# Where and when the second layer's inputs are loaded and split in a two-layer fp32 MLP behind a retention block

## Chip, cores and metric

One core of a Trainium2 chip. The metric is the device time of one execution in microseconds (us), the median of several runs; lower is better.

## What is computed

Attention without a softmax (a decay matrix `Dmat` takes its place), then two feed-forward layers, all in float32. Cut from the reference, with the shapes put in:

```python
q, k, v: [4, 8, 576, 64]
scores = (1 / sqrt(64)) * q @ k.T
ret = scores * Dmat                       # Dmat[h, i, j] = gamma[h] ** (i - j) for i >= j, else 0
x = (ret @ v) -> [2304, 512]
h = x @ w_in                              # first layer, w_in [512, 2048]
x = (h * sigmoid(h)) @ w_out              # w_out [2048, 512]
h = x @ w_in2                             # second layer, the same shapes
out = (max(h, 0) ** 2) @ w_out2           # [2304, 512]
```

## The kernel before

**Tiling.** The 2304 tokens are cut into five blocks (`BLOCKS`: 512, 384, 384, 512, 512). The main loop runs over `(layer, j, f)`: layer 0 with its five blocks `j`, then layer 1 with its five; in each block sixteen steps `f`, one for each group of 128 hidden units. In a step, `gemm1` multiplies the block's input by 128 columns of the first weight into a PSUM tile `ph`; `gate` applies the nonlinearity; `gemm2`, two steps later (`LAG`), adds that group's part into the accumulators `acc`. Every float32 factor is held as a rounded part and a rest (`xh` and `xl`, `gh` and `gl`, `wh` and `wl`), and three products are summed (line 74). A step of a 512-token block is thus 12 matmuls of `gemm1` and 12 of `gemm2`.

**The work beside the matmuls.** For each step ScalarE applies the sigmoid or relu (L380, L383) and casts `gh` (L388); VectorE multiplies (L381, L384) and subtracts `gl` (L389). The weights come as packed 64-bit words `wr`, through three buffers, and are converted by both engines: ScalarE L101, L102 and the cast L121; VectorE L107, L108, L109 and the subtraction L125. `conv_to` works a unit of half a step's weights at a time and mixes three units: while unit i has its L101 and L102, unit i-1 has its L107 to L109, and unit i-2 its L121 and L125. SyncE's queue issues a weight load (L92) as soon as the L109 that frees its buffer is done. The second layer's weights are converted over layer 0's last block and layer 1's first, about nine units in eight steps.

**Order.** Each engine takes its instructions in the order in which the program emits them; it is written out by hand. A function put into `later` is emitted at the next `flush()`, of which there are two in a step, each after a call of `conv_to`. So the gate of a step follows the first of them, the cast of `gh` the second, and the subtraction of `gl` the first of the step after.

**Between the layers.** Each block's output of layer 0 is copied to `y` and written to the DRAM tile `x2[j]` from ScalarE's queue (L433). `load_x2(j)` (lines 435 to 444) reads it back into the tile `xr` from SyncE's queue (L438), and directly behind it emits four ScalarE casts to `xh` (L442) and four VectorE subtractions to `xl` (L443). It is called at step 8 of layer 0's last block for block 0, and at step 4 of each block of layer 1 for the block after it: five calls. `xr` and the output tile `y` share two buffers and take turns in them.

Of the kernel before, what the change touches and what calls it, by code (L numbers as in the profile page):

```python
# [7 lines left out]
F32 = mybir.dt.float32  # L8
F32R = mybir.dt.float32r
# [15 lines left out]
KD, KF = DM // 128, DFF // 128  # L25
BLOCKS = [512, 384, 384, 512, 512]
NBMAX = max(BLOCKS)
LAG = 2
W1_FIRST, W1_AHEAD = 6, 5
ST_W = (0, 1, 1, 2)  # L30
ST_C = (0, 0, 1, 2, 2, 3, 3, 4, 4)
W2_LAG, W2_NUM, W2_DEN = 0, 9, 8
HALF = (slice(0, 64), slice(64, 128))
RAW = 3
# [4 lines left out]
def kernel(  # L39
# [16 lines left out]
    nc = tc.nc  # L56
# [4 lines left out]
    xp = ctx.enter_context(tc.tile_pool(name="xp", bufs=2))  # L61
# [67 lines left out]
    later = []  # L129

    def flush():
        now = later[:]
        later.clear()
        for emit in now:
            emit()
# [5 lines left out]
    def load_next():  # L141
        if n_loaded[0] < load_end[0]:
            load_w(n_loaded[0])
            n_loaded[0] += 1

    def conv_to(layer, n):

        for i in range(conv_n[layer], min(n, 2 * KF + 2)):
            conv_n[layer] += 1
            for lag, stage in ((2, conv_c), (0, conv_a), (1, conv_b), (2, conv_d)):  # L150
                if 0 <= i - lag < 2 * KF:
                    stage(layer * 2 * KF + i - lag)
                    if stage is conv_b and n_loaded[0] < i - lag + layer * 2 * KF + RAW + 1:
                        load_next()
# [200 lines left out]
    x2 = [dp.tile([128, KD, n], F32, name=f"x2_{j}") for j, n in enumerate(BLOCKS)]  # L355
    tok0 = [sum(BLOCKS[:j]) for j in range(len(BLOCKS))]
    late = {}

    def gemm1(layer, j, f):
        n = BLOCKS[j]  # L360
        ph = ps_g.tile([128, 512], F32, tag="g", name="ph")[:, 0:n]
        wh, wl = wt[layer, f]
        xh, xl = x_t[j] if layer == 0 else late["x", j]
        for k in range(KD):
            w0 = slice(k * 128, k * 128 + 128)
            mm3(
                ph,
                [(wh[:, w0], xh[:, k, 0:n]), (wh[:, w0], xl[:, k, 0:n]), (wl[:, w0], xh[:, k, 0:n])],
                first=k == 0,
                last=k == KD - 1,  # L370
            )
        later.append(lambda: gate(layer, j, f, ph))
# [60 lines left out]
                    q.dma_start(out=to, in_=y[:, 0:w])  # L433

    def load_x2(j):
        n = BLOCKS[j]
        r = late["pool"].tile([128, KD, n], F32, tag="xr", name="xr")
        nc.sync.dma_start(out=r, in_=x2[j])  # L438
        xh = xp.tile([128, KD, NBMAX], F32R, tag="xh", name="xh")[:, :, 0:n]
        xl = xp.tile([128, KD, NBMAX], F32R, tag="xl", name="xl")[:, :, 0:n]  # L440
        for k in range(KD):
            nc.scalar.copy(xh[:, k], r[:, k])  # L442
            nc.vector.tensor_sub(xl[:, k], r[:, k], xh[:, k])  # L443
        late["x", j] = (xh, xl)


    nb = len(BLOCKS)
# [34 lines left out]
    def run_att(upto, su=False):  # L482
        while pos[0] < min(upto, len(steps)):
            steps[pos[0]][1](su)
            pos[0] += 1

    def att_end(j):
        last = u_end[j] - 1
        return max(i for i, s in enumerate(steps) if s[0] <= last) + 1

    e0 = att_end(0)
    for i in range(1, e0 + 1):
        run_att(i, True)
        conv_to(0, ST_C[i])
        flush()
# [8 lines left out]
    for i in range(len(seq) + LAG):  # L504
        if i < len(seq):
            layer, j, f = seq[i]
            gemm1(layer, j, f)
        for half in range(2):
            if layer == 0 and j == 0:
                conv_to(0, 2 * f + half + 1 + W1_AHEAD)  # L510
            elif i > w2_base + W2_LAG:
                conv_to(1, (2 * (i - w2_base - W2_LAG) + half - 1) * W2_NUM // (2 * W2_DEN))
            flush()
            if half and i >= LAG:
                gemm2(*seq[i - LAG])
            if i < len(seq) and layer == 0 and j + 1 < nb:
                a0, a1 = att_end(j), att_end(j + 1)
                run_att(a0 + (a1 - a0) * (2 * f + half + 1) // (2 * KF - 3))
        if i < len(seq):
            if layer == 0 and j == nb - 1 and f == 0:  # L520
                ap_ctx.close()
                load_end[0] = 4 * KF
                for _ in range(RAW):
                    load_next()
                late["pool"] = ctx.enter_context(tc.tile_pool(name="lp", bufs=2))
            if layer == 0 and j == nb - 1 and f == KF - 8:
                load_x2(0)
            if layer == 1 and f == 4 and j + 1 < nb:
                load_x2(j + 1)


# [54 lines left out]
```

## Time and profile before

| what | value |
|---|---|
| median of 3 runs | 898.37 us (897.97 to 899.33) |
| the profiled execution's own time | 897.14 us |
| span of its trace | 895.4 us |
| TensorE matmul (PE) busy | 862.8 us, 96% of the span |
| VectorE (DVE) busy | 427.6 us, 48% |
| ScalarE (ACT) busy | 327.1 us, 37% |
| mean granted TensorE clock | 0.982 |

The trace is of one execution, 1.2 us shorter than the median of the runs. Its times count from the start of the span, which leaves 1.7 us of that execution's time outside. PE is TensorE's matmuls, SP is SyncE, which only issues transfers here; SPq and ACTq mark the DMA issues of the two queues. The end of a matmul is modelled in the trace, and neighbours overlap in it; the starts are the better measure.

### The profile page before, as it was taken

How to read it: one execution, taken by the hardware profiler on the slowest of the kernel's cores; microseconds unless marked ns; L12 is line 12 of the kernel's file. 1: busy time of each engine (PE TensorE's matmuls, PEld its weight loads, DVE VectorE, ACT ScalarE, POOL GpSimd, SP SyncE). 2: the span in 40 equal slices, each digit the busy share in tenths (PEclk: the TensorE clock that was granted, in tenths of full speed). 3: DMA queues.
4: the chain of work that ended last, by engine and by line, in shares of the span. 5: the costliest groups of instructions: out<-in, count | busy, mean ns of one | idle time of the engine just before them, and what ended most of it. 6: DMA issues, size and time to landing. Idle time of an engine off the chain costs nothing.

```text
span 895.4 us, 14028 instructions
## 1 busy us (share of the span) xinstructions
PE 862.8 (96%) x5930; PEld 739.8 (83%) x5930; DVE 427.6 (48%) x722; ACT 327.1 (37%) x594; POOL 72.8 (8%) x105
## 2 busy tenths in 40 slices
PE   6698979999999999999999989999999999999998
PEld 5576758999999888888878878889999888888886
DVE  3899995333443333335767776632242233223222
ACT  3576663222222322225556555432232223222221
POOL 5210111111122021100000000000000000000000
PEclk8699999999999999999999999999999999999999
DMA  9445532111211213002343433020020020001001
GB/s 355 175 140 191 181 127 95 48 48 48 84 49 48 84 48 118 1 1 95 120 139 118 142 131 115 2 83 1 1 83 1 0 83 1 1 0 48 1 1 47
DMA packets 21662, 68.27 MB, mean 76 GB/s; under 512 B 2400, under 2 KB 4192, under 8 KB 21216
## 3 DMA queue, kind: packets, MB, share of 16 engines
q1 hardware_dynamic: 17280, 59.91, 19.5%
q10 hardware_dynamic: 4320, 7.47, 2.3%
q8 instruction: 46, 0.75, 0.3%
q14 instruction: 16, 0.13, 0.0%
HBM read 57.93 MB, written 9.44 MB: 75 GB/s over the span
## 4 chain that ended last, share of the span: by engine, by line
PE 82%; DVE 2%; DMA 1%; issue 0%; ACT 0%; SPq 0%; ACTq 0%
PE acc L74 40%; PE ph L74 39%; PE Q L301 2%; DMA xr<-x 1%; PE P L250 1%; PE P L255 1%; DVE xl L443 0%; DVE t L108 0%; DVE gl L389 0%; DVE t L109 0%; DVE t L107 0%; DVE wl L125 0%; PE Q L317 0%; ACT xh L442 0%; SPq L92 0%
## 5 line engine op out<-in xcount | busy, mean ns | idle before, releaser
L74 PE MATMUL ph<-xh,wh 128*128 128x512 f32 (+1 forms) x640 | 238.1, 372 | 5.6 <-ACT xh L335 5.6
L74 PE MATMUL ph<-xl,wh 128*128 128x512 f32 (+1 forms) x640 | 236.4, 369 | 0.0
L74 PE MATMUL ph<-xh,wl 128*128 128x512 f32 (+1 forms) x640 | 236.3, 369 | 0.0
L384 DVE SCALAR_TENSOR_TENSOR sg<-ph,sg 128x512 f32<-128x512 f32 (+1 forms) x80 | 51.0, 638 | 195.3 <-ACT sg L383 195.3
L74 PEld LDWEIGHTS ph<-xh,wh 128*128 128x128 f32 x640 | 120.8, 189 | 24.0 <-ACT xh L335 5.8
L74 PEld LDWEIGHTS ph<-xl,wh 128*128 128x128 f32 x640 | 120.7, 189 | 16.8 <-DVE xl L336 0.4
L74 PEld LDWEIGHTS ph<-xh,wl 128*128 128x128 f32 x640 | 120.7, 189 | 15.2
L74 PE MATMUL acc<-gl,wh 128*128 128x512 f32 (+1 forms) x320 | 120.2, 376 | 9.6 <-DVE gl L389 9.4
L389 DVE TENSOR_TENSOR gl<-sg,gh 128x512 fp32r<-128x512 f32 (+1 forms) x160 | 103.5, 647 | 52.9 <-ACT gh L388 52.6
L388 ACT CAST gh<-sg 128x512 fp32r<-128x512 f32 (+1 forms) x160 | 92.3, 577 | 91.2 <-DVE sg L384 51.5
L381 DVE TENSOR_TENSOR sg<-ph,sg 128x512 f32<-128x512 f32 (+1 forms) x80 | 50.9, 636 | 148.7 <-ACT sg L380 148.7
L74 PE MATMUL acc<-gh,wh 128*128 128x512 f32 (+1 forms) x320 | 120.5, 377 | 0.0
L383 ACT ACTIVATE sg<-ph 128x512 f32<-128x512 f32 (+1 forms) x80 | 44.5, 556 | 207.9 <-PE ph L74 207.5
L74 PE MATMUL acc<-gh,wl 128*128 128x512 f32 (+1 forms) x320 | 119.0, 372 | 0.0
L74 PE MATMUL acc<-wh,gl 128*128 128x512 f32 x288 | 112.8, 392 | 2.8 <-DVE gl L389 2.8
L74 PE MATMUL acc<-wl,gh 128*128 128x512 f32 x288 | 112.6, 391 | 0.0
L74 PE MATMUL acc<-wh,gh 128*128 128x512 f32 x288 | 112.0, 389 | 0.0
L380 ACT ACTIVATE sg<-ph 128x512 f32<-128x512 f32 (+1 forms) x80 | 44.3, 554 | 159.0 <-PE ph L74 159.0
L74 PEld LDWEIGHTS acc<-gl,wh 128*128 128x128 f32 x320 | 60.8, 190 | 21.3 <-DVE gl L389 13.9
L74 PEld LDWEIGHTS acc<-gh,wh 128*128 128x128 f32 x320 | 60.6, 189 | 8.7
L74 PEld LDWEIGHTS acc<-gh,wl 128*128 128x128 f32 x320 | 60.9, 190 | 7.4
L74 PEld LDWEIGHTS acc<-wh,gl 128*128 128x128 f32 x288 | 54.1, 188 | 14.6 <-DVE gl L389 3.2
(50 smaller groups left out, 738.0 us busy)
## 6 DMA issues: line engine op xcount, KB each, us to landing
wr<-w SPq DMA_DIRECT2D x64, 512.0 KB, 3.5
raw<-att SPq DMA_DIRECT2D x34, 512.0 KB, 5.3
x<-y ACTq DMA_DIRECT2D x12, 256.0 KB, 2.5
xr<-x SPq DMA_DIRECT2D x3, 1024.0 KB, 5.5
out<-y SPq DMA_DIRECT2D x10, 256.0 KB, 2.1
out<-y ACTq DMA_DIRECT2D x7, 256.0 KB, 2.3
x<-y ACTq DMA_DIRECT2D x8, 192.0 KB, 1.9
xr<-x SPq DMA_DIRECT2D x2, 768.0 KB, 5.3
```

The lines of the kernel that those rows point to most:

```text
L74: mm(o, a, b, start=first and i == 0, stop=last and i == n - 1)
L250: mm(o, dims(u, a, e, b, 768), dims(u, a, e, b, 0), start=True, stop=True)
L255: mm(o, toks(u, a, e, b, 256), toks(u, a, e, b, 512), start=True, stop=True)
L301: mm(w, a, b, start=e not in started, stop=last)
L380: nc.scalar.activation(s, ph, ACTF.Sigmoid)
L381: nc.vector.tensor_mul(s, ph, s)
L383: nc.scalar.activation(s, ph, ACTF.Relu)
L384: nc.vector.scalar_tensor_tensor(s, ph, 0.0, s, op0=ALU.max, op1=ALU.mult)
L388: nc.scalar.copy(gh, s)
L389: later.append(lambda: nc.vector.tensor_sub(gl, s, gh))
```

## The change

The load is issued from ScalarE's queue in place of SyncE's, at step 4 of the block before (`X2_LOAD`), for block 0 too, where it was step 8. The casts and subtractions are taken out of `load_x2` into `split_x2`, which is called at the end of steps 10 to 13 (`X2_SPLIT`), one cast each; the subtraction goes into `later`, so it is emitted at the first flush of the next step, behind that step's subtraction of `gl`.

```diff
+X2_LOAD, X2_SPLIT = 4, 10
...
     def load_x2(j):
-        n = BLOCKS[j]
-        r = late["pool"].tile([128, KD, n], F32, tag="xr", name="xr")
-        nc.sync.dma_start(out=r, in_=x2[j])
-        xh = xp.tile([128, KD, NBMAX], F32R, tag="xh", name="xh")[:, :, 0:n]
-        xl = xp.tile([128, KD, NBMAX], F32R, tag="xl", name="xl")[:, :, 0:n]
-        for k in range(KD):
-            nc.scalar.copy(xh[:, k], r[:, k])
-            nc.vector.tensor_sub(xl[:, k], r[:, k], xh[:, k])
-        late["x", j] = (xh, xl)
+        r = late["pool"].tile([128, KD, BLOCKS[j]], F32, tag="xr", name="xr")
+        nc.scalar.dma_start(out=r, in_=x2[j])
+        late["r", j] = r
+
+    def split_x2(j, k):
+        n, r = BLOCKS[j], late["r", j]
+        if k == 0:
+            late["x", j] = tuple(
+                xp.tile([128, KD, NBMAX], F32R, tag=nm, name=nm)[:, :, 0:n] for nm in ("xh", "xl")
+            )
+        xh, xl = late["x", j]
+        nc.scalar.copy(xh[:, k], r[:, k])
+        later.append(lambda: nc.vector.tensor_sub(xl[:, k], r[:, k], xh[:, k]))
...
-            if layer == 0 and j == nb - 1 and f == KF - 8:
-                load_x2(0)
-            if layer == 1 and f == 4 and j + 1 < nb:
-                load_x2(j + 1)
+            nxt = j + 1 if layer else 0
+            if (layer == 1 or j == nb - 1) and nxt < nb:
+                if f == X2_LOAD:
+                    load_x2(nxt)
+                if X2_SPLIT <= f < X2_SPLIT + KD:
+                    split_x2(nxt, f - X2_SPLIT)
```

## Rows read from the trace of the kernel before

**Rows 1.** The profile's page: busy time of each engine (share of the span), instructions.

```profile
PE 862.8 (96%) x5930; PEld 739.8 (83%) x5930; DVE 427.6 (48%) x722; ACT 327.1 (37%) x594; POOL 72.8 (8%) x105
```

**Rows 2.** Waits, 440 to 530 us: total us, times, longest us.

```profile
ACT xh L442 <- DMA xr<-x: 12.1, 2, 6.4
DVE xl L443 <- ACT xh L442: 11.4, 2, 6.1
...
PE acc L74 <- DVE gl L389: 4.7, 2, 2.8
```

**Rows 3.** Busy time by stretch, layer 1's second block: us, engines, PEclk, DMA share, GB/s.

```profile
578.00:650.00 72.00, 72.00 (x363) 65.17 (x362) 21.58 (x40) 19.63 (x40) 0.00 (x0) 1.00 0.08 26
```

**Rows 4.** Timeline of PE, first stall: start, us, instruction, idle before and releaser.

```profile
453.99 0.39 PE L74 MATMUL acc<-gh,wh 128*128 128x512 f32 x1
456.24 0.50 PE L74 MATMUL acc<-gl,wh 128*128 128x512 f32 x1 [1.87 <-DVE gl L389]
...
460.46 0.39 PE L74 MATMUL ph<-xh,wh 128*128 128x512 f32 x1
```

**Rows 5.** Timeline of PE, second stall.

```profile
523.04 0.39 PE L74 MATMUL acc<-wh,gh 128*128 128x512 f32 x1
...
526.48 0.50 PE L74 MATMUL acc<-wh,gl 128*128 128x512 f32 x1 [2.83 <-DVE gl L389]
...
528.89 0.39 PE L74 MATMUL ph<-xh,wh 128*128 128x512 f32 x1
```

**Rows 6.** The chain that ended last: an undisturbed group of twelve matmuls.

```profile
463.37 2.72 PE acc L74 x12
```

**Rows 7.** Busy time by stretch, the matmuls right after the first stall.

```profile
458.00:460.46 2.46, 2.46 (x8) 1.89 (x7) 2.46 (x5) 1.85 (x4) 0.00 (x0) 0.56 0.29 40
```

**Rows 8.** Timeline of ACT, at the first stall and at the second.

```profile
452.44 2.18 ACT L442 CAST xh<-xr 128x512 fp32r<-128x512 f32 x4 [6.38 <-DMA xr<-x]
454.53 0.59 ACT L380 ACTIVATE sg<-ph 128x512 f32<-128x512 f32 x1
...
520.92 1.75 ACT L442 CAST xh<-xr 128x384 fp32r<-128x384 f32 x4 [5.75 <-DMA xr<-x]
522.58 0.62 ACT L121 CAST wh<-t 128x512 fp32r<-128x512 f32 x1
```

**Rows 9.** Tile xr: ns min/median/max, first and last start; landing us min/median/max.

```profile
L442 ACT CAST xh<-xr x20: 507/614/620, 452.4 to 740.0; 128x512 fp32r<-128x512 f32 x12, 128x384 fp32r<-128x384 f32 x8
L443 DVE TENSOR_TENSOR xl<-xr,xh x20: 550/684/693, 453.1 to 740.9; 128x512 fp32r<-128x512 f32 x12, 128x384 fp32r<-128x384 f32 x8
L438 SPq DMA_DIRECT2D xr<-x x5: 377/405/469, 446.9 to 724.0; - x5
...
DMA to landing us min/median/max: 4.9/5.5/5.7
```

**Rows 10.** The layer-0 output writes that ScalarE's queue issues: ns min/median/max.

```profile
L433 ACTq DMA_DIRECT2D x<-y x20: 326/327/1324, 152.5 to 503.0; - x20
```

**Rows 11.** Timeline of DVE around step 4 of layer 0's last block.

```profile
424.03 0.69 DVE L109 SCALAR_TENSOR_TENSOR t<-wr,t 128x512 int32<-128x512 int32 x1
...
427.72 0.68 DVE L389 TENSOR_TENSOR gl<-sg,gh 128x512 fp32r<-128x512 f32 x1
...
438.50 0.69 DVE L381 TENSOR_TENSOR sg<-ph,sg 128x512 f32<-128x512 f32 x1 [1.76 <-ACT sg L380]
```

**Rows 12.** Timeline of ACT around the same step.

```profile
421.61 0.60 ACT L380 ACTIVATE sg<-ph 128x512 f32<-128x512 f32 x1 [2.75 <-PE ph L74]
...
430.08 0.68 ACT L101 ACTIVATE t<-wr 128x512 f32<-128x512 f32 x1
```

**Rows 13.** Tile wr, the raw weights: landing us min/median/max of 64 loads.

```profile
DMA to landing us min/median/max: 3.3/3.5/10.8
```

**Rows 14.** Timelines of SP and ACT, the third load and its casts.

```profile
588.21 0.47 SPq L438 DMA_DIRECT2D xr<-x  x1
...
599.86 1.75 ACT L442 CAST xh<-xr 128x384 fp32r<-128x384 f32 x4
```

## Prediction

> **What bounds the kernel now.** I read the page first: matmuls are busy for 96% of the span, the two elementwise engines for less than half [rows 1]. So TensorE sets the end, and the change can only matter where TensorE stands still, or where it makes it stand. The view of waits says where, in the stretch that the diff touches. From 440 to 530 us TensorE waits twice, 4.7 us in all, for a `gl` of VectorE's; in the same stretch VectorE waits twice for the cast `xh` of L442, and ScalarE twice, 12.1 us, for the load of `xr` [rows 2]. That is one chain, read from the bottom up: the transfer is late, ScalarE stands before the first cast, VectorE before the first subtraction, the next step's `gl` is queued behind them, and `gemm2` needs it. In the busy time by stretch, layer 1's second block shows the contrast: a load and a split lie in it too, and TensorE is busy for all 72.00 us at a granted clock of 1.00 [rows 3].
>
> Why only the first two of five calls? They fall into the time in which the second layer's weights are converted. There SyncE reaches the load only after the weight loads ahead of it, each held until L109 frees a buffer, while ScalarE comes to the casts at about the same time. Later no weight load is left: the third load is issued at 588.21 and its casts start at 599.86, 11.65 us later [rows 14], about twice the longest landing of 5.7 us [rows 9]. Those three calls cost TensorE nothing, though they too emit four casts in one go.
>
> **What the two stalls cost.** I measure by the starts of matmuls. Twelve undisturbed ones take 2.72 us [rows 6]. In the first stall, the twelve of one `gemm2` take from 453.99 to 460.46, 6.47 us: 3.75 us too long [rows 4]. Of this 1.87 us is idle [rows 4]; most of the rest is clock, since the matmuls behind the gap show a granted clock of 0.56 from 458.00 to 460.46 [rows 7], so for most of it the lower of the two levels, 1.2 GHz and not 2.4. In the second, twelve take from 523.04 to 528.89, 5.85 us: 3.13 us too long, of which 2.83 us is idle [rows 5]. **The sum is 3.75 + 3.13 = 6.88 us.** Both lie on the path that sets the end, and I find no other wait of TensorE's in the part of the kernel that the diff touches, so this is all that can be won.
>
> **The change, part by part.**
>
> *The load at step 4, casts from step 10.* Six steps of 24 matmuls are 6 x 2 x 2.72 = 32.6 us in a 512-token block, three quarters of it, 24.5 us, in a 384-token one. The load lands in at most 5.7 us [rows 9]. Its wait goes from ScalarE (12.1 us) and with it from VectorE and TensorE: gain 6.88 us. Nothing of this stall has to go elsewhere: the casts' data lies ready some 19 us before it is asked for, and block 0's last cast comes at step 13, three steps before layer 1 needs it.
>
> *The issue from ScalarE's queue.* Five instructions, absent from ScalarE in the trace of before. The nearest rows: SyncE's same issue takes 0.38 to 0.47 us [rows 9], ScalarE's own issue of output writes 0.33 to 1.32 us [rows 10]. I take 0.41, the median of the same transfer. It holds up ScalarE's next gate. What can ScalarE bear? In the first stall it stood from 452.44 - 6.38 to 454.53, 8.47 us, for which TensorE idled 1.87: 6.60 us were free. In the second 5.75 + (522.58 - 520.92) = 7.41 us for 2.83: 4.58 us free [rows 4, 5, 8]. Even 1.32 us is hidden. What the issue itself must wait for (the buffer's last readers, the writes of `x2[j]`) is long past at step 4: the block's writes are two blocks old or more, the buffer's last subtractions some six steps or more. Cost 0, five times.
>
> *SyncE's queue loses the load.* Weight loads behind it (and output writes in layer 1) start up to 0.47 us sooner; no row shows anyone waiting for that. 0.
>
> *One cast and one subtraction a step.* The same 20 casts of 0.51 to 0.62 us and 20 subtractions of 0.55 to 0.69 us [rows 9], now in eight steps with conversion and twelve without. An ordinary step with conversion leaves VectorE 1.76 us idle [rows 11]: one subtraction fits. About one step in eight has two weight units between its gates. Step 4 to 5 is such a place, and by the ratio of 9 units to 8 steps the next is step 12 to 13, inside the new split. There the `gl` of step 4 is ready at 427.72 + 0.68 = 428.40 [rows 11]; its `ph` was done at 421.61 [rows 12], and its `gemm2` starts four groups later, at 421.61 + 4 x 2.72 = 432.5. That leaves 4.1 us; two subtractions before it, were none of them absorbed, would take 1.4. Cost 0, with 1.4 us per block as the far bound if that cover were gone.
>
> *Sharing with the weight loads.* This is the one thing that could bite. At step 4 the weight load freed by L109 at 424.03 + 0.69 = 424.72 is wanted by L101 at 430.08, two units on [rows 11, 12]: 5.36 us of lead against a landing of 3.5 [rows 13]. The load of `xr` now comes from another queue at just that moment. If all of it goes first, the weights land after 3.5 + 5.5 = 9.0 us, 3.6 late, within the 4.58 that ScalarE can bear. Cost 0. The far bound takes the longest landing, 10.8 [rows 13], and adds 5.5: 16.3 us, 10.9 late, 6.4 us of stall at each of the two loads that meet conversions.
>
> The Trainium skill, "DMA: Bandwidth & Descriptors", section "Issuing engines are not separate DMA queues", speaks against expecting anything of the new queue: transfers from different engines end on the same 16 DMA engines and interleave, and issuing from several saves only the issuing time. By that rule the gain here is all in the six steps, none in the queue, and the weight loads lose their place ahead of `xr`. The sum by it is the same 6.88 us as long as the weights' lateness stays under what ScalarE can bear.
>
> **The rivals.**
>
> *Weight loads late (slower).* Place: steps 4 to 6 of layer 0's last block and of layer 1's first. L101 stands before a late weight load, and the gates are queued behind it on ScalarE. For it: the lead of only 5.36 us, and the page's rule of interleaving. Against it: the trace has landings of 10.8 us at most, in a kernel that starts with many transfers in flight. It decides when both weight loads land later than 5.36 + 4.58 + 3.44 = 13.4 us; at the far bound, 16.3, the time is 898.37 - 6.88 + 12.8 = 904.3. Landings from 9.9 to 13.4 only eat the gain.
>
> *The spread splits push `gl` back at the steps with two units.* For it: VectorE has no idle time there. Against it: 4.1 us of slack. Price up to 1.4 us at each of two blocks: 892 to 894.3.
>
> *The change does not do what it says.* ScalarE might stand at its own issue, or the casts at step 10 might still wait, so that the stall only changes its place. For it: ScalarE's issues have taken 1.32 us. Against it: 24 us or more between issue and first cast. The time would be about 898.4 with both stalls kept, 895 with one.
>
> **Numbers.** Against the profiled execution: 897.14 - 6.88 = 890.26. It lies 1.23 us below the median of the runs shown; from the median, 898.37 - 6.88 = **891.5 us**, which I forecast for the median after. Full gain: 87%. Splits that push `gl`: 4%. Stall kept in part or whole: 4%. Weight loads late: 3% with part of the gain eaten, 2% slower. The range goes from 889.9 (the profiled execution's figure less the 0.4 us by which the fastest run lay under the median) to 893.8 (891.5, plus 0.96 for the slowest run shown, plus one block's 1.4). A change under 0.2%, 1.8 us, can hardly be told from none for this kernel; faster than that, under 896.6, takes in the full gain, the pushed `gl` and most of the partial cases: 95%. Within it 3%, slower 2%.
>
> **What would show it.** In the profile after: no wait of ScalarE's cast for `xr`, and none of TensorE for `gl` in the second half; the granted clock 1.00 across layer 0's last block; the issue on ScalarE near 0.4 us; L101 waiting for `wr` for at most some 4 us near step 5; VectorE's waits for L442 short. It would be wrong if a new wait of TensorE's shows at steps 4 to 6 (weights) or 12 to 15 (`gl`), or if clock is lost where no gap is.

## The result, and the profile after

890.81 us against 898.85 us (medians of four runs each, beside one another): 8.0 us less, a ratio of 0.9912 with a 95% interval of 0.9895 to 0.993. The forecast was 891.5 us in a range of 889.9 to 893.8, and faster. The two profiled executions differ by 6.0 us (897.14 and 891.10), their spans by 6.1.

The page after, as in [rows 1]:

```profile
span 889.3 us, 14027 instructions
...
PE 860.3 (97%) x5930; PEld 738.6 (83%) x5930; DVE 428.1 (48%) x722; ACT 327.3 (37%) x594; POOL 72.9 (8%) x105
```

The waits after, for the stretch of [rows 2]. The whole answer has no row of TensorE's and none for `xr`; its first rows are the gates that wait for their matmuls:

```profile
ACT sg L381 <- PE ph L75: 13.6, 7, 2.7
ACT sg L384 <- PE ph L75: 11.4, 7, 2.7
DVE sg L385 <- ACT sg L384: 10.5, 6, 2.4
```

Busy time by stretch after: layer 0's last block, and layer 1's first. TensorE is busy without a gap in both, at the full granted clock (compare [rows 7]):

```profile
399.80:487.00 87.20, 87.20 (x386) 72.24 (x385) 60.78 (x101) 49.06 (x87) 0.00 (x0) 1.00 0.35 117
487.00:578.00 91.00, 91.00 (x407) 75.95 (x406) 62.57 (x105) 48.45 (x87) 0.00 (x0) 1.00 0.30 100
```

The tile `xr` after, as in [rows 9]: the issue takes 0.33 us on ScalarE's queue, the load lands in 4.0 to 4.8 us.

```profile
L439 ACTq DMA_DIRECT2D xr<-x x5: 326/332/333, 423.6 to 731.6; - x5
...
DMA to landing us min/median/max: 4.0/4.8/4.8
```

Timeline of ScalarE after, at step 4 of layer 0's last block, as in [rows 12]:

```profile
423.23 0.68 ACT L102 ACTIVATE t<-wr 128x512 f32<-128x512 f32 x1
423.59 0.33 ACTq L439 DMA_DIRECT2D xr<-x  x1
423.81 0.68 ACT L103 ACTIVATE wr<-wr 128x512 int32<-128x512 uint32 x1
424.38 0.61 ACT L389 CAST gh<-sg 128x512 fp32r<-128x512 f32 x1
...
430.70 0.67 ACT L102 ACTIVATE t<-wr 128x512 f32<-128x512 f32 x1
```

The issue falls inside the conversion's instructions and costs ScalarE no gap: from this step's gate to the conversion below it are 8.48 us (422.22 to 430.70), against 8.47 in [rows 12]. The weight conversion that I feared for stands at 430.70 without a wait. This trace's matmuls run 0.6 us later than those of before already ahead of the change (the gate of this step starts at 422.22, against 421.61 in [rows 12]), so from there on 6.1 + 0.6 = 6.7 us were won in this pair, near the 6.88 that I took.

### The profile page after: what moved, and what is told of

Its sections match the earlier page's. It is cut to its first block, busy times and chain, and to the rows that moved or that the text cites. A ratio compares the mean times of both kernels' runs of the same rounds, so it can differ in the third digit from the quotient of the medians.

```text
span 889.3 us, 14027 instructions
## 1 busy us (share of the span) xinstructions
PE 860.3 (97%) x5930; PEld 738.6 (83%) x5930; DVE 428.1 (48%) x722; ACT 327.3 (37%) x594; POOL 72.9 (8%) x105
## 4 chain that ended last, share of the span: by engine, by line
PE 84%; DVE 0%; issue 0%; ACT 0%
PE acc L75 41%; PE ph L75 40%; PE Q L302 2%; PE P L251 1%; PE P L256 1%; PE Q L318 0%; DVE t L109 0%; DVE wl L126 0%; DVE S L287 0%; DVE gl L390 0%; DVE y L429 0%; ACT y L427 0%; DVE t L108 0%; DVE t L110 0%
```

## The experiments

A theory is needed for what the stalls were. The forecast's: ScalarE stands too long for a late load, and it can bear only 6.60 and 4.58 us. Later a second one: ScalarE's standing hardly matters; the four differences `xl` stood on VectorE ahead of a `gl` that was due.

**e1_sync_queue: the queue undone.**

```diff
-        nc.scalar.dma_start(out=r, in_=x2[j])
+        nc.sync.dma_start(out=r, in_=x2[j])
```

> The changed kernel with one part undone: the load at step 4 goes out from SyncE's queue again, casts and differences stay one per step from step 10. Theory (the load was asked for too late; which queue asks does not matter): SyncE reaches it at most one weight unit, about 5 us, after step 4, it lands two or more steps before step 10, no wait of ScalarE's for xr, same time as the changed kernel, about 890.8 us, ratio to before 0.991. Rival (leaving SyncE's queue is what pays): the load stands behind weight loads again, ScalarE waits several us at step 10 and TensorE about 3 us at each of two loads: 895 to 898 us, ratio 0.996 to 1.000.

Measured: 890.92 us, ratio 0.9919 [0.9902, 0.9936]. No wait for `xr`, none of TensorE's behind 390 us. SyncE reaches the first load at 426.36, 3.7 us after its step's gate, where ScalarE in the changed kernel took 1.4; the five loads land in 5.1 to 5.8 us. The queue is not what pays in the changed kernel.

**e2_burst_at_10: the spreading undone.**

```diff
-                if X2_SPLIT <= f < X2_SPLIT + KD:
-                    split_x2(nxt, f - X2_SPLIT)
+                if f == X2_SPLIT:
+                    for k in range(KD):
+                        split_x2(nxt, k)
...
-        later.append(lambda: nc.vector.tensor_sub(xl[:, k], r[:, k], xh[:, k]))
+        nc.vector.tensor_sub(xl[:, k], r[:, k], xh[:, k])
```

> The changed kernel with one part undone: all four casts, each directly followed by its difference, are emitted in one go at step 10; load early and from ScalarE's queue as in the changed kernel. Theory (lateness alone cost time): ScalarE is held for 1.7 to 2.2 us, less than the 4.58 us that it can bear, TensorE does not wait, about 890.8 us, ratio 0.991. Rival (the burst itself costs, the spreading pays): TensorE waits 1 to 2 us for gl in each of the two blocks with weight conversion: 893 to 895 us, ratio 0.994 to 0.996.

Measured: 890.78 us, 0.992 [0.9901, 0.9938], no wait of TensorE's. With the data there, four differences ahead of `gl` cost 2.4 us on VectorE, which `gl` has to spare. Nor is the spreading needed, then, once the load is early.

**e3_queue_only: the queue alone, on the kernel before.**

```diff
-        nc.sync.dma_start(out=r, in_=x2[j])
+        nc.scalar.dma_start(out=r, in_=x2[j])
```

> The kernel before with one part of the change: the load goes out from ScalarE's queue, at the old place, with its four casts and differences directly behind it. Theory (what counts is how long ScalarE stands between issue and casts): it stands for landing and casts, 4.8 + 2.2 = 7.0 us at the first load and 4.1 + 1.8 = 5.9 us at the second, against 6.60 and 4.58 us that were free: TensorE idles 0.4 and 1.3 us, with up to 2 us more where the clock falls; at the three later loads ScalarE stands for 5.9 to 7.0 us as well, where before it did not, but no conversions share the engines there and TensorE does not wait. 892.5 to 895 us, ratio 0.993 to 0.996. Rival (the queue is what pays): as the changed kernel, 890.8 us. Second rival (a wait at every load costs): three new stalls of TensorE, 898 us or more.

Measured: 892.3 us, 0.9937 [0.992, 0.9954]: the stated time just missed, at its lower end. But the stalls are not where they were expected. ScalarE stands for `xr` at all five loads, 19.2 us in all, and TensorE waits neither at the first nor, but for 0.1 us, at the second. It waits at the fourth call, in a 384-token block without conversions. Timeline of PE there:

```profile
667.32 0.40 PE L74 MATMUL acc<-wl,gh 128*128 128x512 f32 x1
668.74 0.50 PE L74 MATMUL acc<-wh,gl 128*128 128x512 f32 x1 [1.02 <-DVE gl L389]
```

Timeline of ScalarE, at the first load and at the second:

```profile
444.68 0.33 ACTq L438 DMA_DIRECT2D xr<-x  x1
449.61 2.18 ACT L442 CAST xh<-xr 128x512 fp32r<-128x512 f32 x4 [3.53 <-DMA xr<-x]
451.70 0.59 ACT L380 ACTIVATE sg<-ph 128x512 f32<-128x512 f32 x1
...
514.25 1.76 ACT L442 CAST xh<-xr 128x384 fp32r<-128x384 f32 x4 [2.84 <-DMA xr<-x]
515.92 0.61 ACT L121 CAST wh<-t 128x512 fp32r<-128x512 f32 x1
```

ScalarE stands 5.6 us at the first load (from 446.08 to 451.70) and 4.5 us at the second (from 511.41 to 515.92), less than the 7.0 and 5.9 us expected, because the issue starts about 1.4 us before ScalarE has nothing else to do. Both lie under the forecast's 6.60 and 4.58 us, so neither speaks against it. The fourth call does speak against the expectation: conversions are not what makes a load cost.

**e4_before_again: the kernel before, unchanged, for a second trace.**

> The kernel before once more, nothing changed, for a second trace of it. The medians fell by 8.0 us, the profiled executions by 6.0, and the forecast was 6.88. Theory (the size of the two stalls differs from one execution to the next, through the clock after them): this trace shows the same two idle gaps of about 1.9 and 2.8 us but more matmuls at the lower clock behind them, or the like gap at the start, 1 to 2 us more in all. Rival (the difference lies elsewhere): the same 6.9 us for the two stalls within 0.3 us, and the surplus in the first 135 us. Ratio 1.000.

Measured: 898.67 us over 12 runs, from 895.2 to 901.25; ratio 1.0 [0.9985, 1.0014]. The same two stalls in PE's timeline, as in [rows 4, 5]:

```profile
454.14 0.39 PE L74 MATMUL acc<-gh,wh 128*128 128x512 f32 x1
456.51 0.64 PE L74 MATMUL acc<-gl,wh 128*128 128x512 f32 x1 [1.99 <-DVE gl L389]
...
460.72 0.39 PE L74 MATMUL ph<-xh,wh 128*128 128x512 f32 x1
...
523.28 0.39 PE L74 MATMUL acc<-wh,gh 128*128 128x512 f32 x1
...
526.85 0.50 PE L74 MATMUL acc<-wh,gl 128*128 128x512 f32 x1 [2.95 <-DVE gl L389]
...
533.58 0.39 PE L74 MATMUL acc<-wh,gh 128*128 128x512 f32 x1
```

First: 460.72 - 454.14 - 2.72 = 3.86 us lost, as before. Second, over 24 matmuls: 533.58 - 523.28 - 5.44 = 4.86 us, against 3.13. Together 8.72 instead of 6.88, and the span is 1.9 us longer. The busy time by stretch, behind the second gap, says why: here the clock fell there too.

```profile
529.60:532.00 2.40, 2.40 (x8) 1.89 (x7) 2.37 (x5) 1.59 (x4) 0.00 (x0) 0.54 0.63 205
```

The theory of a varying clock held. And VectorE's timeline at the first stall shows something that I had read wrongly:

```profile
446.48 0.68 DVE L125 TENSOR_TENSOR wl<-t,wh 128x512 fp32r<-128x512 f32 x1
453.36 2.50 DVE L443 TENSOR_TENSOR xl<-xr,xh 128x512 fp32r<-128x512 f32 x4 [6.19 <-ACT xh L442]
455.77 0.69 DVE L389 TENSOR_TENSOR gl<-sg,gh 128x512 fp32r<-128x512 f32 x1
```

The `gl` at 455.77 is that of the load's own step, 8, whose cast on ScalarE was done before ScalarE began to stand. It sat in `later` while `load_x2` emitted the four `xl` ahead of it. The first trace of this kernel, that of [rows 8], has the same order: on ScalarE the cast of `gh` directly ahead of the casts that wait, and on VectorE, at the second stall, the four `xl` and then a weight unit (L107 to L125, from 523.35) ahead of `gl`:

```profile
445.45 0.61 ACT L388 CAST gh<-sg 128x512 fp32r<-128x512 f32 x1
...
521.47 1.97 DVE L443 TENSOR_TENSOR xl<-xr,xh 128x384 fp32r<-128x384 f32 x4 [5.34 <-ACT xh L442]
...
525.75 0.68 DVE L389 TENSOR_TENSOR gl<-sg,gh 128x512 fp32r<-128x512 f32 x1
```

From here on the second theory was tested.

**e5_order_only: the kernel before, the differences put into `later`.**

```diff
-            nc.vector.tensor_sub(xl[:, k], r[:, k], xh[:, k])
+            later.append(lambda k=k: nc.vector.tensor_sub(xl[:, k], r[:, k], xh[:, k]))
```

> The kernel before with one word of the change: the four differences xl go into later, so that each is emitted behind the difference gl of the step in which the load is called; queue, place of the load and the four casts in a row stay, and ScalarE still stands for xr. Theory formed from the traces (TensorE stood for the gl of the load's own step, whose cast was long done, only because that difference was queued on VectorE behind the four xl): at the first load gl goes through at once and TensorE does not wait; at the second gl still stands behind a weight difference L125 whose cast L121 is behind the four casts on ScalarE, and is ready about 1.0 us late; 891.5 to 893.7 us, ratio 0.992 to 0.995. Rival (ScalarE's standing for a late load is the cost, as the forecast had it, with 6.60 and 4.58 us that it can bear): ScalarE stands 8.5 and 7.4 us as before, TensorE idles 1.9 and 2.8 us, 897 to 899 us, ratio 0.998 to 1.001.

Measured: 892.23 us, 0.9933 [0.9917, 0.9949]: inside the theory's range, far from the rival's. ScalarE waits for `xr` as long as ever, 12.3 us. VectorE's timeline, at the first load and at the second:

```profile
447.76 0.68 DVE L389 TENSOR_TENSOR gl<-sg,gh 128x512 fp32r<-128x512 f32 x1
454.01 2.50 DVE L443 TENSOR_TENSOR xl<-xr,xh 128x512 fp32r<-128x512 f32 x4 [5.57 <-ACT xh L442]
...
520.37 0.69 DVE L125 TENSOR_TENSOR wl<-t,wh 128x512 fp32r<-128x512 f32 x1 [5.31 <-ACT wh L121]
520.98 0.68 DVE L389 TENSOR_TENSOR gl<-sg,gh 128x512 fp32r<-128x512 f32 x1
521.58 1.96 DVE L443 TENSOR_TENSOR xl<-xr,xh 128x384 fp32r<-128x384 f32 x4
```

At the first, `gl` goes through while ScalarE stands, and TensorE does not wait. At the second it is behind a weight difference that needs ScalarE, and TensorE idles 1.0 us, as worked out beforehand; behind 400 us this is its only wait:

```profile
PE acc L74 <- DVE gl L389: 1.0, 1, 1.0
```

One reordering of four instructions gives 6.0 of the 7.6 us that e6 gives.

**e6_spread_only: the changed kernel, load back in SyncE's queue and at its old, late step.**

```diff
-X2_LOAD, X2_SPLIT = 4, 10
+X2_AT = (KF - 8, 4)
...
-        nc.scalar.dma_start(out=r, in_=x2[j])
+        nc.sync.dma_start(out=r, in_=x2[j])
...
-                if f == X2_LOAD:
+                if f == X2_AT[layer]:
...
-                if X2_SPLIT <= f < X2_SPLIT + KD:
-                    split_x2(nxt, f - X2_SPLIT)
+                if X2_AT[layer] <= f < X2_AT[layer] + KD:
+                    split_x2(nxt, f - X2_AT[layer])
```

> The changed kernel with the load back in SyncE's queue and at its old step (8 for block 0, 4 for the others), the first cast in the same step as the load; only the spreading is left: one cast per step, each difference behind gl. Theory (own gl behind the differences): ScalarE stands 6 us for xr at the first two loads, but gl is not held behind the differences; TensorE waits 0 to 0.3 us; 890.6 to 892 us, ratio 0.991 to 0.993. Rival (ScalarE's standing is the cost): it stands 6.9 and 6.2 us with one cast, against 6.60 and 4.58 us that it can bear, TensorE idles 0.3 and 1.6 us and loses clock: 893 to 895 us, ratio 0.994 to 0.997.

Measured: 890.57 us, 0.9916 [0.9898, 0.9934]: the full gain. The waits show the late load in full, and no row of TensorE's behind 400 us:

```profile
ACT xh L449 <- DMA xr<-x: 12.3, 2, 6.5
```

ScalarE stands as long for `xr` as in [rows 2], with one cast behind each wait and not four, and it costs nothing.

**e7_hold18 and e10_hold12: how long ScalarE may be held.** The changed kernel; 12 is in place of 18 in the second.

```diff
         xh, xl = late["x", j]
+        if k == 0 and j < 2:
+            for _ in range(18):
+                nc.scalar.copy(xh[:, k], r[:, k])
```

> The changed kernel with ScalarE held on purpose: at step 10 in the two blocks with weight conversion, the first cast is done 18 times more, into the same place with the same values, so that ScalarE is busy for 9.4 + 0.5 us there and 7.6 + 0.4 us in the second. Theory (a held ScalarE delays only the gates of the next step, whose gl is due 10.9 us after its gemm1; the own gl passes): ScalarE can bear about 10 us, TensorE idles 0 to 1 us in all, 890.5 to 892.5 us, ratio 0.991 to 0.993. Rival (the 6.60 and 4.58 us of the forecast are what ScalarE can bear): TensorE idles 3.3 and 3.4 us and loses clock, 897 to 900 us, ratio 0.999 to 1.002.

> The changed kernel with ScalarE held at step 10, as in the run with 18 repeated casts, but 12 of them: by the 0.65 and 0.54 us that one took there, ScalarE is busy for 8.3 us in the first block and 6.9 us in the second. There it was busy 12.3 us and TensorE idled 2.9, so 9.4 us were free. Theory (with the own gl past, ScalarE can bear about 9.4 us): no wait of TensorE's, 890.3 to 891.5 us, ratio 0.990 to 0.993. Rival (6.60 and 4.58 us, as the forecast had it): TensorE idles 1.7 and 2.3 us and may lose clock, 894.5 to 898 us, ratio 0.996 to 1.000.

Measured with 18: 897.49 us, 0.9993 [0.998, 1.0005], a miss of the time that my theory gave. Two things were off. The repeated casts took 0.65 us each and not 0.52, so ScalarE was busy from 457.30 to 469.60, 12.3 us and not 9.9; and what TensorE then waited for was mostly not `gl` but a free `ph`, which the late gate holds: 2.9 us in the first block, and in the second 0.8 us for `ph` and 0.6 for `gl`. Timelines of ScalarE and of PE:

```profile
457.30 11.74 ACT L451 CAST xh<-xr 128x512 fp32r<-128x512 f32 x18
469.07 0.62 ACT L452 CAST xh<-xr 128x512 fp32r<-128x512 f32 x1
469.60 0.59 ACT L381 ACTIVATE sg<-ph 128x512 f32<-128x512 f32 x1
...
471.07 0.80 PE L75 MATMUL ph<-xh,wh 128*128 128x512 f32 x1 [2.91 <-DVE sg L382]
```

From the first block, 12.3 - 2.9 = 9.4 us can be borne ahead of that wait. These 4.3 us of idle time are less than the 6.7 by which the run is slower than the changed kernel; the granted clock was 0.50 behind the first gap. With 12: 891.4 us, 0.993 [0.9917, 0.9944], as the theory had it; ScalarE is held from 457.63 to 465.99, 8.4 us, and of TensorE's waits behind 440 us this is all:

```profile
PE acc L75 <- DVE gl L390: 0.3, 1, 0.3
```

**e8_more_dma and e9_twice_the_load: the rival of late weight loads, priced.** The changed kernel; the first issues copies that nothing reads ahead of the load (`spare` are DRAM tiles), the second one more load into a spare SBUF buffer behind it. The lines that declare these tiles are left out.

```diff
+        if j < 2:
+            for i in range(6):
+                nc.scalar.dma_start(out=spare[j, i], in_=x2[j])
         nc.scalar.dma_start(out=r, in_=x2[j])
```

```diff
         nc.scalar.dma_start(out=r, in_=x2[j])
+        if j < 2:
+            e = late["ex"].tile([128, KD, BLOCKS[j]], F32, tag="ex", name="ex")
+            nc.scalar.dma_start(out=e, in_=x2[j])
```

> The changed kernel with more traffic where the load goes out: ahead of each of the first two loads ScalarE's queue issues six copies of the same block from DRAM to DRAM (6 MB and 4.5 MB), which nothing reads. It prices the rival of late weight loads. If the two queues share the DMA engines, a weight load of 0.5 MB gets its half and lands in 4 to 6 us, L102 waits for it at most 1 us, TensorE does not wait: 890.5 to 892 us, ratio 0.991 to 0.993 (xr lands late, some 17 to 30 us after step 4, still before or about step 10). If the earlier traffic goes first, as the forecast's far bound had it, the weight loads land over 15 us after their issue, ScalarE stands 10 us or more for them in both blocks, and TensorE idles 5 us or more: over 900 us.

> The changed kernel with the suspected traffic doubled in its own kind: at step 4 of the two blocks with conversion ScalarE's queue issues a second load of the same block from DRAM into a spare SBUF buffer that nothing reads. The copies of the run before this one went in packets of 64 KB (6.29 MB in 96), the load of xr goes in packets of 8 KB, the weights in 4 KB. Theory (a single load of xr is far from making the weights late): a weight load lands some 1 to 3 us later than the 3.5 us, L102 waits for it at most 2.5 us, TensorE does not wait: 890.3 to 891.5 us, ratio 0.990 to 0.993. Rival (weights wait until both loads are through): they land 9.5 us and more after their issue, L102 waits 4 to 6 us and more, TensorE idles up to 2 us in each of the two blocks: 892 to 896 us.

The copies: 905.39 us, 1.0083 [1.0059, 1.0108], so 7 us slower than before, and against my expectation. A weight load lands after 22.6 us at the longest; in ScalarE's timeline a conversion behind the copies waits for one:

```profile
445.57 0.66 ACT L102 ACTIVATE t<-wr 128x512 f32<-128x512 f32 x1 [11.54 <-DMA wr<-w]
```

and TensorE idles 7.4 and 2.9 us for `ph`. Part of it is ScalarE's own: from the first copy's issue at 423.07 to the load's at 429.46 its queue is taken, and its next cast of a weight starts at 429.89, where the changed kernel has it at 425.42. The copies go in far larger packets than the load does (the expectation of e9 has the figures), so this run shows that the rival's mechanism exists, not what a load of `xr` does. From 430 to 442 us the two queues move 32 packets each in every 3 us, but ScalarE's (q10) eight times the bytes of SyncE's (q1). The Trainium skill, "DMA: Bandwidth & Descriptors", section "Queues, rings and completion order", says that a DMA engine takes turns between the queues by whole packets; by that rule a queue with 64 KB packets gets most of the engine from one with 4 KB packets, and this trace agrees with that. So neither of my two expectations held, neither half of the bytes for the weights nor all copies first. The DMA view of 430 to 433 us, packets, MB and share of the 16 engines:

```profile
q10 hardware_dynamic: 32, 1.05, 91.3%
q1 hardware_dynamic: 32, 0.13, 11.8%
```

Twice the load: 891.0 us, 0.9925 [0.991, 0.994], as expected. L102 waits 1.4 us for a weight load at the first doubled load (below) and 0.2 us at the second, and TensorE does not wait:

```profile
ACT t L102 <- DMA wr<-w: 1.4, 1, 1.4
```

**e11_flush_first: the same cure for the waits that are left.** The changed kernel, in the main loop:

```diff
         for half in range(2):
+            flush()
             if layer == 0 and j == 0:
                 conv_to(0, 2 * f + half + 1 + W1_AHEAD)
             elif i > w2_base + W2_LAG:
                 conv_to(1, (2 * (i - w2_base - W2_LAG) + half - 1) * W2_NUM // (2 * W2_DEN))
-            flush()
```

> The changed kernel with flush() ahead of conv_to in each half step of the main loop, so that a step's gl, and its gate, go ahead of the weight conversion of that half and not behind it: the same cure (no gl behind work that is not yet due) for the waits of TensorE's that are left, 7.5 us for gl in the first 160 us. Theory: half or more of these waits go, the weights are converted 1 to 2 us later and are still in time: 885 to 889 us, ratio 0.985 to 0.990. Rival (VectorE is busy without a gap there, so the wait only moves from gl to the weights): 890 to 893 us, ratio 0.990 to 0.995.

Measured: 894.44 us, 0.9964 [0.9951, 0.9976]: 3.6 us above the changed kernel's 890.81, worse than the rival's range too. TensorE's waits for `gl` in the first 160 us are 9.5 us instead of 7.5:

```profile
PE acc L75 <- DVE gl L390: 9.5, 8, 2.4
```

The surplus is in the first of the eight, 2.42 us in place of 0.45; the seven behind it are as long as in the changed kernel, to within 0.05 us, each 2.3 us later. VectorE is busy for 75.1 us of the 80 from 60 to 140 us in both kernels, and there the order changed nothing. What it cost shows in VectorE's timeline ahead of the first wait: with the flush first, the first gate stands ahead of two weight units, and VectorE stands for it, where in the changed kernel it converts those units from 36.24 to 41.20 us.

```profile
41.42 0.69 DVE L382 TENSOR_TENSOR sg<-ph,sg 128x512 f32<-128x512 f32 x1 [4.69 <-ACT sg L381]
```

So here it was the weight units that were ready, and the gate that was not. No run was measurably faster than the changed kernel.

## Why the prediction was right, and where its account was wrong

**The sum.** Both stalls went, nothing took their place, and the kernel gained what they cost. Of the two terms, 3.75 us repeated in the second trace (3.86). The 3.13 us of the second stall seems mis-sized for the median: there the clock may fall as well, and then it is 4.86. The profiled execution of before happened to be one without that; two traces do not show which is the commoner. From the median of this comparison 6.88 would have given 892.0 us and the second trace's 8.72 gives 890.1; the measured 890.81 lies between. The sum was of measured stalls and the change takes away the lateness itself, so it came out without the right mechanism.

**The cause.** My chain ran "VectorE stands before the first subtraction, the next step's `gl` is queued behind them". The step was wrong in one word: it was the `gl` of the load's own step, which is due one step, 5.4 us, earlier and did not depend on ScalarE any more. What followed from it fell with it, namely that ScalarE "can bear" 6.60 and 4.58 us. Held 8.4 us it costs 0.3 us of idle time (e10), and standing as long as before for a late load it costs nothing (e6), as long as the `xl` do not stand ahead of `gl` and the casts come one per step. With all four casts in one go a part of the chain was as I had it, at the second load only: there `gl` stood behind a weight difference that needed ScalarE, for 1.0 us (e5). The 6.60 and 4.58 measured how late the four `xl` may come, and only in those two steps.

**What in the change gives the gain.** Either of two things does it: the load asked for early (e2, from ScalarE's queue, four casts in a row, `xl` ahead of `gl`; the same from SyncE's queue was not run), or the differences one per step behind `gl` (e6, load late and in SyncE's queue). The queue by itself gives 6.2 us of it (e3): ScalarE's queue does not have the weight loads ahead, so the first load is issued at 444.68, 2.2 us before SyncE reached it at 446.9 [rows 9], and the loads land in 4.9 us at most, against 5.7. With an early load and the spreading it adds nothing (e1). "By that rule the gain here is all in the six steps, none in the queue" was right about the queue in the changed kernel. It was wrong about the queue at the old step (e3), and about the six steps, for which the order of the differences can stand in.

**The costs that I put at nothing** were nothing. ScalarE's issue took 0.33 us (I took 0.41), and it did not hold up ScalarE's next gate, as I had it. At the place with two weight units, step 12 to 13, VectorE's timeline after has the `gl` of step 12 from 471.85 to 472.54; its gate started at 465.74, so it was due at 465.74 + 4 x 2.72 = 476.6, and 4.1 us were left, as worked out:

```profile
471.85 0.69 DVE L390 TENSOR_TENSOR gl<-sg,gh 128x512 fp32r<-128x512 f32 x1
```

The weights were not late: even twice the load made L102 wait only 1.4 us, where my bound for one load had 3.6 us late. A stall of the size of the far bound, 6.4 us, came only with traffic of another kind (7.4 and 2.9 us, e8).

**The rivals.** Late weight loads: real as a mechanism, but seen only with 6.3 MB of copies in larger packets (e8). Splits that push `gl` back: no. The change that does not do what it says: no.

## What to carry to other kernels

In an engine's queue, look behind a waiting instruction for work that was ready and due; putting the late work behind it (four differences, e5) was worth most of what making the late work early was: 6.0 us, against 7.8 in e2. It is no rule to put every due instruction first: in e11 the instruction put first was not ready, and the kernel lost 3.6 us against the changed one. A wait in the profile is named after what came last, so read the timeline of the waiting engine, and ask for each instruction in it which step it belongs to, before pricing how long an engine may be held. And a stall of TensorE costs its idle time plus a clock that may or may not fall behind it: one trace shows one draw of that.

## What was unexpected of the hardware

- **The clock behind a gap varies.** After gaps of 1.87 and 1.99 us the granted clock fell to its lower level (0.50) within about a microsecond, and after one of 2.91 us in e7 it was there at once. After one of 2.83 us it stayed at 1.00, and after one of 2.95 us it fell only some 1.5 us later. So the length of the gap alone does not say here what follows it. The kernel before ran from 895.2 to 901.3 us in 12 runs, the one without from 890.5 to 891.5 in four; most of the spread of the kernel before may be this, but only the two traces show it. Busy time by stretch, behind the gaps of 1.99 (e4), 2.83 ([rows 5]) and 2.91 us (e7), one line each:

```profile
456.50:458.50 2.00, 1.99 (x5) 1.60 (x6) 1.93 (x4) 1.65 (x3) 0.00 (x0) 0.55 0.00 0
...
526.48:528.90 2.42, 2.42 (x11) 2.00 (x12) 2.35 (x5) 1.84 (x4) 0.00 (x0) 1.00 0.50 201
...
471.10:474.00 2.90, 2.90 (x7) 2.32 (x8) 2.83 (x6) 2.90 (x7) 0.00 (x0) 0.50 0.14 16
```

- **A DMA issue on ScalarE's queue ran beside its computing.** In the timeline after it stands at 423.59, ahead of the cast of `gh` at 424.38 that the program emits before it, and no instruction of ScalarE's is delayed. So here ScalarE's order held for what it computes, and the DMA issue ran ahead of that. Six issues in a row did hold it up (e8).
- **Eighteen casts into one place took 0.65 us each**, where the four casts of a split take 2.18 us together, 0.55 each.
